# A planned attention kernel: a latest end per slot for fillers and products with v, and eight more homes for VectorE's exponentials

## The chip, the cores and the metric

The kernel runs on one core of one Trainium2 chip. The metric is the device time of one execution in microseconds (us). The engines are TensorE (PE in the profile), VectorE (DVE), ScalarE (ACT), GpSimd (POOL) and SyncE (SP), which issues most DMAs.

## The reference

The inputs are x (2048 x 640), wqkv, wo, w1, b1, w2 and gate_w, all bf16. The layer mixes a 32-head softmax attention (head size 20) with a dense Mish layer by a gate for each row:

```python
g = sigmoid((x * gate_w).sum(-1, keepdims=True))
a = softmax_attention(x, wqkv, heads=32, scale=20 ** -0.5) @ wo
h = x @ w1 + b1
b = (h * tanh(softplus(h))) @ w2
out = g * a + (1 - g) * b
```

## The kernel before, in words

Scores are computed transposed: for a chunk of 512 queries (four chunks c), a group of four heads (eight groups g) and a tile of 128 keys (sixteen tiles kt), each head j gives one unit, a 128 x 512 tile of scores. There are 2048 units in an order that is fixed by `groups`: chunks 0 and 1 alternate group by group, then come chunks 2 and 3. The last group is cut in two halves of 256 queries.

Three units make a slot, and there are 683 slots. The scores of a slot fill three PSUM banks, and two such sets of banks alternate, so the scores of slot s+2 (`emit_s`, matmuls on line 1061) can start once ScalarE has read slot s. ScalarE takes the exponential of a whole slot in one instruction (`emit_e`, line 1083) into one of five ETS buffers. In some slots the third unit is not ScalarE's: VectorE computes its exponential by a polynomial in four instructions (`emit_x`: line 1111 reads the scores, then two on line 1127 and one on line 1129). Such a slot has a narrow instruction on ScalarE (1024 columns instead of 1536); the dictionary `off` holds these slots. The result of such a unit lies in a *home* until TensorE has multiplied it by v. `home()` picks the one that has been free for longest, out of three in a work area of W2R or REG, two in XE and, early on, four lent ones in HB and XS (`LENT`). `ei(home)` gives the address of one. `choose(s)` decides for each slot whether VectorE takes its third unit: not if there is no free home, if VectorE is too far behind, or if its result would come too late for its group; the first slot that may be chosen for is set by `CALM`.

TensorE also makes the products with v (`pv`, line 1197), which add up in the bank ACC, one pass for each key tile; `emit_pv` issues them in order, at most two passes in a step. In between come tasks that share the bank FB: projections for K, Q and v (lines 541, 607, 705, 732), the two matrices of the dense layer (lines 851 and 910), the output projection (line 934), and a check of the score range (line 774). They are cut into single matmuls and run by due times; those called forced must be through by their due step. At the end `spin` (line 1471) and `repeat_s` add matmuls without a purpose where TensorE would stand too idle (`fill_up`). Normalised results of chunks 0 and 1 lie in the tile OTN, those of chunks 2 and 3 in the columns of QT that are no longer needed.

No order on any engine is decided on the chip. A planner in Python (class `Plan`) adds one instruction after the other with an assumed cost, keeps a clock for each engine, and derives the waits from the dependencies. The main loop goes slot by slot: forced tasks, the exponential of the slot, the scores of slot s+2, fillers for the clock, VectorE's unit, then products with v, then tasks up to `limit`, then fillers again. In this loop `limit` is the time by the planner's clock until which tasks may run:

```python
limit = pl.now["act"] + EXP + HOP if step < NSLOT else 1e9
owed = min(owed + rate, 1.0) if step < NSLOT else 1e9
...
emit_pv(step, 2 if step < NSLOT - 1 else 99)
```

`emit_pv` itself knew no limit in time. A second program for large scores is built behind a flag and does not run with these inputs.

Of the kernel before, what the change touches and what calls it, by code (L numbers as in the profile page):

```python
# [10 lines left out]
I32 = mybir.dt.int32  # L11
# [36 lines left out]
SWITCH = 0.1  # L48
COL = 1 / 2400.0
PASS = CW * COL  # L50
EXP = 1.335
STREAM = 0.48
SPUN = 0.6
EXP_PAIR = 0.908
# [24 lines left out]
LAG = 9  # L79
SPARE = 3.5  # L80
WINDOW = 3.41
CALM = 4
PACKED = 10
PACKED_Q = 12
Q_AT = 100
# [3 lines left out]
H_AT = 150  # L89
H_STEP = 12.5  # L90
THIN = 0.09
OVER = 0.2
CUTS = ((0, 256), (256, 256))

# [124 lines left out]
def bass_gated_mix__softmax_full_mha__dense_activation_mish__prompt_kernel(  # L219
# [35 lines left out]
    OTN = sb("OTN", [P, 2, NG, CW], BF16)  # L255
# [26 lines left out]
    def ball(tb):  # L282


        at = XS[:, :] if tb < 2 else XB[:, (tb - 2) // 4, (tb - 2) % 4 // 2 * 2 * D:][:, 0:2 * D]
        return at[:, (tb % 2) * D:(tb % 2 + 1) * D]
# [23 lines left out]
    def ei(home):  # L310

        area, b = home
        if area == "h":
            return HB[:, 1, 4 * b:4 * b + 4, :].rearrange("p f t -> p (f t)").bitcast(I32)
        if area == "x":
            return XS[:, 0:2 * CW].bitcast(I32)
        return XE[:, b - 3, :] if b >= 3 else AREAS[area][1][:, b * CW:(b + 1) * CW]

    def otn(c, g, fast):
# [14 lines left out]
    NSLOT = -(-NC * NG * NKT * HG // SLOT)  # L334


    off = {}
    off_units = {}

    def attention(pl, fast):  # L340
# [3 lines left out]
        at = {}  # L344
# [80 lines left out]
        def flush(done):  # L425

            while not done():
                ready = [lane for lane in soon if lane]
                first = min(ready, key=lambda lane: (lane[0][2]().t1 if lane[0][2] else 0.0, lane[0][3]))
                first.popleft()[1]()  # L430
# [24 lines left out]
        otn_read = {0: [], 1: []}  # L455
# [493 lines left out]
        def of(half):  # L949
            return slice(half * HALF, (half + 1) * HALF)  # L950
# [18 lines left out]
        def p_task(c, t, half, due, rest=False):  # L969

            tb = c * 4 + t
            some = late if rest else every
            needed = [g for g in some if g < NG - 1]
            needed.append(next((k[1] for k, (at, w) in cut.items() if k[0] == c and at <= t * P < at + w), NG - 1))

            def ready():
                if any((c, g) not in otn_done for g in needed) or (fast and (tb, half) not in bdone):
                    return None
                if fast and len(wog_ready) < 2 * HG + 1 or rest and (t, half) not in part_done:
                    return None  # L980
                return [otn_done[(c, g)] for g in needed] + wog_ready

            def finish(bank, last):
                otn_read[c % 2].append(last)
                add = PART[:, t, half, :] if rest else ball(tb)[:, of(half)]
                if rest:
                    ev = mix(ended(t, half), bank, tb, add, [last, part_done[(t, half)]])
                    give(t, half, ev)
                    return ev
                ev = mix(OUTT[:, :], bank, tb, add, [last, bdone.get((tb, half)), *out_dma.values()])  # L990
                store(tb, half, ev)
                return ev

            return Task([p_mm(c, t, half, g, some) for g in some], HALF * COL, finish, due, ready)
# [22 lines left out]
        ei_free = {(a, b): None for a in range(2) for b in range(3)}  # L1017
        ei_free.update({(None, b): None for b in range(3, UNITS)})
        ei_free.update({at: None for at in LENT})
        given_back = set()  # L1020
        area = [0]
        nx = [0]
        off_home = {}
# [2 lines left out]
        started = {}  # L1026
        queue = deque()
        hold = {"until": 0}
        acc_free = [m_acc if fast else pl.add("dve", lambda e: e.memset(PS[:, ACC, :], 1.0))]

        def compose(s, extra=None):
# [19 lines left out]
        def score_mms(s, some, deps):  # L1051

            op = None
            for r in range(max(len(subs(*u[:3])) for u in some)):
                began = False
                for i, (c, g, kt, j) in enumerate(some):
                    if r >= len(subs(c, g, kt)):
                        continue
                    tile, cols, of_q = subs(c, g, kt)[r]
                    cost = max(extent(c, g)[1] * COL, THIN)  # L1060
                    op = pl.add("pe", lambda e, i=i, g=real(g), tile=tile, j=j, cols=cols, c=c, of_q=of_q: e.matmul(  # L1061
# [36 lines left out]
        def home():  # L1098

            some = [(None if b >= 3 else area[0], b) for b in range(UNITS)]  # L1100
            some += [at for at in LENT if at[0] not in given_back]
            some = [at for at in some if ei_free[at] != "busy"]
            return min(some, key=lambda at: ei_free[at].t1 if ei_free[at] else 0.0, default=None)

# [98 lines left out]
        def emit_pv(step, passes):  # L1203

            while passes and step >= hold["until"]:
                if not queue:
                    return
                c, g, kt, _ = queue[0][2]
                emit_off((c, g), False)
                n = HG - sum(u[2] == kt for u in off_units.get((c, g), ()) if fast)  # L1210
                if len(queue) < n:
                    return
                if kt == tiles(c, g) - 1 and not emit_off((c, g), True):
                    if step < NSLOT - 1:
                        return
                    flush(lambda: emit_off((c, g), True, True))
                passes -= 1
                some = [queue.popleft() for _ in range(n)]
                lasts = pv([(u, ETS[:, s % NETS, i, :], [e_op[s]]) for s, i, u in some])
                for k, (s, i, u) in enumerate(some):  # L1220
                    op = pv_slot[s] = lasts[k]
                    pv_left[s] -= 1
                if kt == tiles(c, g) - 1:
                    hold["until"] = step + PV_HOLD
                    group_done(c, g, step, op)
# [70 lines left out]
        if fast:  # L1296
# [60 lines left out]
            for make, args in rest:  # L1357
                t = make(*args, 0)
# [131 lines left out]
        for step in range(NSLOT + 40):  # L1490
            now["step"] = step
            if step >= NSLOT and not queue and not tasks and not any(k >= step for k in at):
                break

            for t in [t for t in tasks if t.forced and t.due <= step]:
                while now["open"] not in (None, t):
                    put(now["open"])
                while t in tasks:
                    put(t)
            if step < NSLOT:  # L1500
                emit_e(step)
            if fast and area[0] and not w2_load and len(h_done) >= FIRST and all(ei_free[(0, b)] != "busy" for b in range(3)):
                load_w2()
            if acts and safe(acts[0][0]) < pl.now["act"] and mish_free():
                acts.popleft()[1]()
            ahead = able = 0.0
            rate = behind = 0.0
            lag = max((step - t.due for t in tasks if not t.forced and t.ready() is None), default=0)
            for t in tasks:
                slack = max(1, t.due - AHEAD * t.forced - step)  # L1510
                ahead += t.left()
                rate = max(rate, ahead / slack)
                if t.forced or t is now["open"] or t.ready() is not None:
                    able += t.left()
                    behind = max(behind, able / slack)
            now["rate"] = rate
            if step + 2 < NSLOT:
                compose(step + 2, choose(step + 2) if fast and step >= CALM and (step < slot_of(0, 1, 0) or behind < CATCH_UP and (lag < LAG or backlog() < SPARE) and room()) else None)
                emit_s(step + 2)
                to_come = pv_ready() * PASS  # L1520
                if owed + rate > 0.1 and pick(pl.now["pe"] + 0.8):
                    to_come += min(owed + rate, 0.4)
                fill_up(to_come, False)

                if fast and step + 2 in off:
                    emit_x(step + 2)
            limit = pl.now["act"] + EXP + HOP if step < NSLOT else 1e9
            owed = min(owed + rate, 1.0) if step < NSLOT else 1e9
            if fast and step < NSLOT and now["open"] and now["open"].left() <= min(owed + OVER, limit - pl.now["pe"] - PASS - SWITCH):
                t = now["open"]  # L1530
                while t in tasks:
                    put(t)
                    owed -= t.cost
            emit_pv(step, 2 if step < NSLOT - 1 else 99)

            while owed > 0:
                t = pick(limit)
                if t is None:
                    break
                put(t)  # L1540
                owed -= t.cost
            fill_up(0.0, True)
            for fn in at.pop(step, []):
                fn()
            work(pl.now["act"] + 0.5 if step < NSLOT else 1e9)
        assert not queue and not tasks and not bg and not any(soon) and not norm and not blend and not acts, (len(queue), len(tasks), len(bg), len(acts))

        c = NC - 1
# [109 lines left out]
    fast = Plan("f_")  # L1658
# [55 lines left out]
```

## Time and profile before

| what | value |
|---|---|
| median of 3 runs | 866.54 us (866.3 to 866.74) |
| the profiled execution | 866.43 us |
| its span, first to last instruction | 864.6 us |
| TensorE busy | 756.3 us (87%) |
| VectorE busy | 829.4 us (96%) |
| ScalarE busy | 847.8 us (98%) |
| wide exponentials (128 x 1536) | 454 |
| narrow exponentials (128 x 1024) | 229, of which 228 by VectorE's units and one the last, short slot |
| products with v, score matmuls, spins | 1875 on ETS, 2202, 103 |

Busy time is the union of an engine's instructions. A releaser, written `<-`, is what ended an engine's idle time just before an instruction. The profiled execution's own time is 1.8 us above its span.

### The profile page before, as it was taken

Reading aid. Unit: us, or ns where it says so; the run is one execution under the profiler, and the core shown is the slowest. Engines: PE = TensorE matmul, PEld = TensorE weight load, DVE = VectorE, ACT = ScalarE, POOL = GpSimd, SP = SyncE. Lnnn points to the kernel's source line nnn. Section 1 sums busy time; section 2 is a strip of 40 time slices with the busy share of each in tenths; the row PEclk is TensorE's granted clock in tenths of the full one; section 3 lists DMA queues with packets and bytes.
Section 4 is the critical chain, followed back from the end, with each engine's and each line's share of the span. In section 5 each row is a group of like instructions: output and inputs, shape, how many; then the busy total and the mean of one; then the engine's idle time right before and its main releaser. Section 6 shows DMA issues by size and latency. Waiting matters only on the chain.

```text
span 864.6 us, 15494 instructions
## 1 busy us (share of the span) xinstructions
PE 756.3 (87%) x6342; PEld 259.5 (30%) x6342; DVE 829.4 (96%) x1330; ACT 847.8 (98%) x714; POOL 7.3 (1%) x14
## 2 busy tenths in 40 slices
PE   8988998889889888898888888898888888899886
PEld 3333332223322332232223333333322333333232
DVE  4799999999999999999999999999999999999996
ACT  6999999999999999999999999999999999999996
POOL 2000000000000000000000000000000000000000
PEclk9999999999999999999999999999999999999999
DMA  9711310012233221401111211112112211000001
GB/s 215 95 61 36 107 46 19 16 60 69 78 93 89 67 62 53 123 26 38 44 39 44 71 34 58 44 36 60 55 44 60 59 51 41 28 25 29 18 14 35
DMA packets 76318, 48.42 MB, mean 56 GB/s; under 512 B 22104, under 2 KB 71888, under 8 KB 76192
## 3 DMA queue, kind: packets, MB, share of 16 engines
q1 hardware_dynamic: 73872, 46.86, 20.1%
q8 instruction: 52, 0.85, 0.4%
q10 hardware_dynamic: 2256, 0.47, 0.3%
q0 software_dynamic: 112, 0.01, 0.1%
q14 instruction: 26, 0.21, 0.1%
HBM read 37.64 MB, written 7.52 MB: 52 GB/s over the span
## 4 chain that ended last, share of the span: by engine, by line
ACT 94%; PE 4%; DMA 1%; DVE 0%; issue 0%; SPq 0%
ACT ETS L1083 92%; ACT REG L884 2%; PE PS L1061 1%; PE PS L1197 1%; ACT W2R L884 1%; DMA OTN<-in_A_x_dram 1%; PE PS L607 0%; PE PS L910 0%; PE PS L670 0%; DVE HB L940 0%; PE PS L774 0%; PE PS L679 0%; PE PS L851 0%; PE PS L541 0%; PE PS L1471 0%
## 5 line engine op out<-in xcount | busy, mean ns | idle before, releaser
L1083 ACT ACTIVATE ETS<-PS 128x1536 bf16<-128x1536 f32 (+1 forms) x683 | 827.6, 1449 | 1.9 <-PE PS L1061 1.7
L1061 PE MATMUL PS<-QT,KT 32*128 32x512 bf16 (+1 forms) x2202 | 275.8, 377 | 95.3 <-ACT ETS L1083 82.7
L1197 PE MATMUL PS<-ETS,V_all 128*21 128x512 bf16 (+1 forms) x1875 | 212.3, 379 | 0.7 <-DVE OUNG L1275 0.4
L1061 PEld LDWEIGHTS PS<-QT,KT 32*128 32x128 bf16 x2202 | 68.4, 91 | 308.9 <-ACT ETS L1083 280.8
L1127 DVE SCALAR_TENSOR_TENSOR ER<-ER 128x512 f32<-128x512 f32 x114 | 77.9, 683 | 0.1
L1127 DVE SCALAR_TENSOR_TENSOR EM<-EM 128x512 f32<-128x512 f32 x114 | 77.7, 682 | 0.0
L1197 PEld LDWEIGHTS PS<-ETS,V_all 128*21 128x21 bf16 x1875 | 48.4, 89 | 92.9 <-issue 84.6
L910 PE MATMUL PS<-W2R,HB 128*128 128x320 bf16 x384 | 74.4, 302 | 0.4
L1111 DVE TENSOR_SCALAR REG<-PS 128x512 f32<-128x512 f32 x85 | 58.2, 685 | 1.9 <-PE PS L1061 1.0
L851 PE MATMUL PS<-XB,REG 128*128 128x256 bf16 x360 | 57.5, 275 | 1.5 <-DVE HB L861 0.9
L1111 DVE TENSOR_SCALAR XE<-PS 128x512 f32<-128x512 f32 x78 | 53.3, 686 | 5.3 <-PE PS L1061 4.3
L910 PEld LDWEIGHTS PS<-W2R,HB 128*128 128x128 bf16 x384 | 28.1, 97 | 38.6 <-issue 27.4
L851 PEld LDWEIGHTS PS<-XB,REG 128*128 128x128 bf16 x360 | 27.9, 97 | 29.1 <-issue 27.2
L861 DVE TENSOR_TENSOR HB<-PS,B1T 128x512 bf16<-128x512 f32 x48 | 32.8, 684 | 1.1 <-PE PS L851 0.9
L1471 PE MATMUL PS<-KT 128*128 128x512 bf16 x103 | 32.0, 385 | 0.0
L1127 DVE SCALAR_TENSOR_TENSOR EM<-REG 128x512 f32<-128x512 uint16 x43 | 29.4, 684 | 0.3
L1129 DVE SCALAR_TENSOR_TENSOR REG<-EM,REG 128x512 int32<-128x512 f32 x43 | 29.3, 681 | 0.0
L1127 DVE SCALAR_TENSOR_TENSOR ER<-REG 128x512 f32<-128x512 uint16 x42 | 28.7, 684 | 0.2
L1129 DVE SCALAR_TENSOR_TENSOR REG<-ER,REG 128x512 int32<-128x512 f32 x42 | 28.6, 681 | 0.0
L1127 DVE SCALAR_TENSOR_TENSOR EM<-XE 128x512 f32<-128x512 uint16 x39 | 26.8, 686 | 0.3
L1127 DVE SCALAR_TENSOR_TENSOR ER<-XE 128x512 f32<-128x512 uint16 x39 | 26.7, 686 | 0.3
L1129 DVE SCALAR_TENSOR_TENSOR XE<-EM,XE 128x512 int32<-128x512 f32 x39 | 26.6, 683 | 0.1
(136 smaller groups left out, 813.1 us busy)
## 6 DMA issues: line engine op xcount, KB each, us to landing
REG<-in_B_w_dram SPq DMA_DIRECT2D x36, 320.0 KB, 3.1
BCT<-SUMS SPq DMA_DIRECT2D x31, 256.0 KB
W2R<-in_B_w_dram SPq DMA_DIRECT2D x12, 320.0 KB, 3.2
KT<-KS SPq DMA_DIRECT2D x28, 128.0 KB
QT<-QS SPq DMA_DIRECT2D x112, 20.0 KB
QS<-WOQ SPq DMA_DIRECT2D x16, 128.0 KB, 1.7
KS<-OTN SPq DMA_DIRECT2D x16, 128.0 KB, 1.7
W2R<-in_B_w_dram SPq DMA_DIRECT2D x1, 1920.0 KB, 9.2
```

The costliest lines, as they stand in the source:

```text
L851: return lambda e, bank: e.matmul(PS[:, bank, i * HW:(i + 1) * HW], w1b(n1)[:, f, i * P:(i + 1) * P], xt(c)[:, f, cols], start=(f == 0), s ...
L861: ev = dve(lambda e: e.tensor_tensor(hb, PS[:, bank, :].rearrange("p (i t) -> p i t", i=2), bias, ALU.add), [last, b_load, *guarded, *b_re ...
L884: ex = pl.add("act", lambda e: e.activation(U, h, AF.Tanh, scale=0.5, bias=-MISH_AT / 2), [ev, u_free[0]], cost=0.95)
L910: return lambda e, bank: e.matmul(PS[:, bank, 0:HALF], HB[:, hc % 2, f, t * P:(t + 1) * P], W2[:, f, half * HALF:(half + 1) * HALF], start ...
L1061: op = pl.add("pe", lambda e, i=i, g=real(g), tile=tile, j=j, cols=cols, c=c, of_q=of_q: e.matmul(scores(s)[:, i, cols], KT[32 * j:32 * j ...
L1083: e_op[s] = pl.add("act", lambda e: e.activation(ETS[:, s % NETS, 0:n, :], scores(s)[:, 0:n, :], AF.Exp, scale=SCALE, bias=LIFT if fast el ...
L1111: ev_op[s] = dve(lambda e: e.tensor_scalar(y, scores(s)[:, 2, :], SCALE * ULPS, BIAS, ALU.mult, ALU.add), [s_op[s], ei_free[b], *(wkv_read ...
L1127: piece(WIDE, lambda e, v=m if i else f, i=i: e.scalar_tensor_tensor(m, v, STEPS[i], v, ALU.add, ALU.mult), lambda i=i: () if i else [lane ...
L1129: piece(WIDE, lambda e: e.scalar_tensor_tensor(x, m, LAST_STEP, y, ALU.mult, ALU.add))
L1197: lasts[n] = pl.add("pe", lambda e, tile=tile, h=real(g) * HG + j, j=j, src=src[:, cols], of_q=of_q, count=count: e.matmul(PS[32 * j:32 * ...
L1471: pl.add("pe", lambda e: e.matmul(PS[:, bank, :], k[:, 0:P], k, start=True, stop=True), [free], cost=PASS, kind="S")
```

## The change

Three edits are made together. `CALM` goes from 4 to 3, so VectorE's units may be chosen one step earlier. A new variable `latest` is set in each step to the planner's time at which the two exponentials after this one will have ended, less `REFILL` = 0.58 us; `limit` is cut to it, and `emit_pv` stops before a pass that would end later. Once all eight output projections of chunk 0 (or 1) have read its half of OTN, four areas in this half join the homes, as `("o", b)`.

```diff
-CALM = 4
+CALM = 3
...
+REFILL = 0.58
...
+        if area == "o":
+            return OTN[:, b // 4, b % 4 * 2:b % 4 * 2 + 2, :].rearrange("p g t -> p (g t)").bitcast(I32)
...
             def finish(bank, last):
                 otn_read[c % 2].append(last)
+                if fast and c < 2 and len(otn_read[c]) == 8:
+                    gained.extend(("o", 4 * c + i) for i in range(4))
+                    ei_free.update({at: last for at in gained[-4:]})
...
+        gained = []
...
+        latest = [1e9]
...
             some += [at for at in LENT if at[0] not in given_back]
+            some += gained
...
+                if passes < 50 and pl.now["pe"] + PASS + (SWITCH if pl.kind != "V" else 0) > latest[0]:
+                    return
                 passes -= 1
...
             limit = pl.now["act"] + EXP + HOP if step < NSLOT else 1e9
+            latest[0] = 1e9
+            if fast and step + 2 < NSLOT:
+                latest[0] = pl.now["act"] + sum(EXP_PAIR if s in off else EXP for s in (step + 1, step + 2)) - REFILL
+                limit = min(limit, latest[0])
```

In the program as built, ScalarE has 228 narrow exponentials instead of 229, VectorE 227 units instead of 228, 52 of them with a home in OTN; TensorE has 21 score matmuls fewer and one spin more, and the same products with v and tasks; the counts of DMAs are the same.

## The prediction

> **What bounds the kernel.** I read the page first.
>
> ```profile
> span 864.6 us, 15494 instructions
> ...
> PE 756.3 (87%) x6342; PEld 259.5 (30%) x6342; DVE 829.4 (96%) x1330; ACT 847.8 (98%) x714; POOL 7.3 (1%) x14
> ...
> ACT 94%; PE 4%; DMA 1%; DVE 0%; issue 0%; SPq 0%
> ```
>
> ScalarE (ACT) is busy for 98% of the span and carries 94% of the chain that ended last. So the time is ScalarE's work, plus what ScalarE loses to others, plus some 10 us ahead and 9 behind. Next the chain of waits in order of time, for the ends of the exponential stream, and ScalarE's groups with shapes kept apart.
>
> ```profile
> 10.33 8.17 ACT ETS L1083 x6
> ...
> 412.27 1.45 ACT ETS L1083
> ...
> 855.99 0.04 issue
> ...
> 859.10 1.00 DVE HB L940 x2
> ```
>
> ```profile
> L1083 ACT ACTIVATE ETS<-PS 128x1536 bf16<-128x1536 f32 x454 | 649.3, 1585 | 1.2 <-PE PS L1061 1.0
> L1083 ACT ACTIVATE ETS<-PS 128x1024 bf16<-128x1024 f32 x229 | 252.5, 1181 | 0.7 <-PE PS L1061 0.7
> L884 ACT ACTIVATE REG<-HB 128x1024 f32<-128x1024 bf16 x18 | 21.5, 1193 | 0.0
> L884 ACT ACTIVATE W2R<-HB 128x1024 f32<-128x1024 bf16 x6 | 7.1, 1178 | 0.0
> ```
>
> The mean durations are not the price of one: neighbours overlap. ScalarE's timeline around twelve wide exponentials in a row gives the price.
>
> ```profile
> 671.04 1.11 ACT L884 ACTIVATE REG<-HB 128x1024 f32<-128x1024 bf16 x1
> 671.99 16.28 ACT L1083 ACTIVATE ETS<-PS 128x1536 bf16<-128x1536 f32 x12
> 687.96 1.25 ACT L884 ACTIVATE REG<-HB 128x1024 f32<-128x1024 bf16 x1
> ```
>
> The first row ends at 672.15, the second at 688.27: 16.12/12 = 1.343 us from end to end. From start to start it is only (687.96-671.99)/12 = 1.331; starts creep ahead of ends. The third row ends at 689.21, so a mish step costs 0.94. For the narrow one I take a run of 50 without a break (its timeline row, then its counts by shape):
>
> ```profile
> 108.07 59.16 ACT L1083 ACTIVATE ETS<-PS 128x1536 bf16<-128x1536 f32 x50 [0.29 <-PE PS L1061]
> ```
>
> ```profile
> L1083 ACT ACTIVATE ETS<-PS 128x1536 bf16<-128x1536 f32 x31 | 46.8, 1653 | 0.3 <-PE PS L1061 0.3
> L1083 ACT ACTIVATE ETS<-PS 128x1024 bf16<-128x1024 f32 x19 | 22.8, 1250 | 0.0
> ```
>
> After a gap a wide one takes 1.45 by itself (the row at 412.27), so 59.16 - 1.45 - 30 x 1.343 = 17.42 for 19: 0.917 each. A narrow one is a slot whose third tile VectorE computes; it spares ScalarE 1.343 - 0.917 = 0.426 us.
>
> The stream runs from 10.33 to 855.99, 845.66 us. Its work is 454 x 1.343 + 229 x 0.917 + 24 x 0.94 = 842.3, with 0.1 for one small instruction; the first exponential starts fresh, another 0.1. So ScalarE loses about **3.2 us** to TensorE in the whole span, and no more can be won by removing late scores. Of it, 1.9 - 0.5 (before the first) = 1.4 is shown as idle in the two group rows, some nine restarts at 0.11 each (1.45 - 1.343) are 1.0, and the rest is slots that start only slightly late.
>
> That ends and not starts count, I checked against the Trainium skill, Perfetto Trace Analysis, section "DVE / Act Engine Instruction": a reported end is where the semaphore update is pushed, a start only where the ALUs begin. The trace agrees, since score groups start 0.05 us after an end (below). By the starts the stream would have lost about 10 us.
>
> **Where the 3.2 us arise.** One loss in the timeline of all engines, then TensorE's timeline around another.
>
> ```profile
> 106.46 1.33 ACT L1083 ACTIVATE ETS<-PS 128x1024 bf16<-128x1024 f32 x1
> ...
> 107.63 0.60 PE L1061 MATMUL PS<-QT,KT 32*128 32x512 bf16 x6
> ...
> 108.07 4.13 ACT L1083 ACTIVATE ETS<-PS 128x1536 bf16<-128x1536 f32 x3 [0.29 <-PE PS L1061]
> ...
> 109.58 0.39 PE L1061 MATMUL PS<-QT,KT 32*128 32x512 bf16 x3 [0.36 <-ACT ETS L1083]
> ```
>
> ```profile
> 583.10 0.39 PE L1061 MATMUL PS<-QT,KT 32*128 32x512 bf16 x3 [0.50 <-ACT ETS L1083]
> 583.42 0.40 PE L1197 MATMUL PS<-ETS,V_all 128*21 128x512 bf16 x4
> 583.74 0.72 PE L851 MATMUL PS<-XB,REG 128*128 128x256 bf16 x5
> 584.40 0.39 PE L1061 MATMUL PS<-QT,KT 32*128 32x512 bf16 x3
> ```
>
> In the first, two narrow exponentials have just passed; scores start at 107.63, the exponential 0.44 later at 108.07, ending the first of its three at 109.52; the next scores follow that end by 0.05. Loss: the three end at 112.20, the one before ended at 107.79, and 4.41 - 3 x 1.343 = 0.38.
>
> This gives a rule. Scores of slot b can start when the exponential of b-2 has ended, and no loss arises if they start 0.44 + 1.45 = 1.89 ahead of the time at which the exponential of b would end in an unbroken stream. Between the starts of the scores of b-1 and b there may then lie: the two exponentials b-2 and b-1, plus one wide (1.343), less 1.89, less 0.05. With one narrow and one wide that is 1.66 us, after a **pair** of narrow ones 0.917 x 2 + 1.343 - 1.94 = **1.23 us**. TensorE's rows: a score group 0.32 to the next instruction, a pass with v 0.32, five filler matmuls 0.66. The second fence is such a pair with all three: 584.40 - 583.10 = 1.30, a loss of 0.07.
>
> I laid this on TensorE's order of instructions as built, with these durations. Before: 77 pairs, 21 overfull, excess 2.3 us; no gap that isn't behind a pair is overfull. Carrying lateness on through runs of three and four gives 2.9 of the 3.2.
>
> **The change, part by part.**
>
> *The latest end* (REFILL). A product pass with v and a filler are now refused where they would end later than the two next exponentials less 0.58 us. The rule above puts the point at 2 x 0.917 + 1.343 - 1.89 = 1.29 after the earlier exponential, where the cap has about 2 x 0.91 - 0.58 = 1.24: the cap lies just inside. What is refused is done one slot later. TensorE has the room:
>
> ```profile
> PE PS L1061 <- ACT ETS L1083: 82.7, 226, 1.1
> ```
>
> It waits 82.7 us for ScalarE in 226 places. Queued behind a refused pass are the later passes with v and through them the reuse of the five ETS buffers; ScalarE's waits name only L1061, never L1197, so that cover exists now. SP, GpSimd and the DMAs keep their counts.
>
> In the changed order I find 65 pairs, 2 overfull, excess 0.5 us: one at the start, one near slot 171. The first is also there now:
>
> ```profile
> 20.39 0.82 PE L541 MATMUL PS<-XB,REG 128*128 128x512 bf16 x3
> ...
> 21.58 2.39 ACT L1083 ACTIVATE ETS<-PS 128x1024 bf16<-128x1024 f32 x2 [0.33 <-PE PS L1061]
> ```
>
> It is a K task with a due step, which the cap does not touch; its 0.33 + 0.11 stays. So the walk falls from 2.9 to 0.5: **-2.4**. Of the 0.3 that the walk does not explain I take half: **-0.1**, between 0 and -0.3.
>
> *CALM 4 to 3.* The choice of a unit may begin a step earlier. In the new order the first four narrow slots stand behind five wide ones instead of six, and their number is the same, so it moves only the opening; between -0.4 (the whole loss at 21.58) and +0.4 (as much again); I take 0.
>
> *More homes.* Eight areas of 128 x 512 words in the tile OTN join the pool, four as soon as the output projection (L934) of a chunk has read its half.
>
> ```profile
> L934 PE MATMUL PS<-WOQ,OTN x128: 299/299/311, 449.7 to 613.0; 128*128 128x320 bf16 x128
> ```
>
> They come free between these times. A unit is one L1111, which takes it from the scores, and three more instructions of the same size:
>
> ```profile
> L1111 DVE TENSOR_SCALAR REG<-PS 128x512 f32<-128x512 f32 x85 | 58.2, 685 | 1.9 <-PE PS L1061 1.0
> ```
>
> With OTN as home no such row exists; the nearest is the one with REG, 685 ns, and I take that; VectorE isn't on the chain, so a few ns either way move nothing by themselves. In the new order 52 of the units live in OTN. But units are not won by it: 227 instead of 228, since three edits together move every later choice. One slot fewer is narrow: **+0.43** on ScalarE. The homes buy spacing: 12 fewer pairs, counted above.
>
> *Fillers for the clock.* 21 score matmuls fewer (17 wide, 4 half; the repeats are among them) and one spin more, on TensorE, beside ScalarE. The tail behind 855.99 hangs on VectorE's last normalisation and the last projections, in the same order in both; four of five spins leave it, and one earlier projection with its eviction (L940, half a us by the row at 859.10) comes into it, ahead of the last three. Between 0 and +0.5; I take 0, as it stands where VectorE waits for TensorE anyway.
>
> Sum: -2.4 - 0.1 + 0.43 = **-2.1 us**. The profiled execution took 866.43 (its span and 1.8 around it), the median of three is 866.54, 0.1 more. I give 864.4, as 866.43 less 2.1 is 864.3 and the median stands 0.1 above. Own range: the unexplained part, the opening and 0.2 of spread make it 863.8 to 865.1.
>
> **Rivals.**
>
> *Half comes back.* What is refused makes a later slot overfull, or a fetch of keys lands late where the order has moved. For it: the sum rests on a walk in which all durations are medians, and 0.3 us of the present loss escapes it. Against it: the 82.7 us of room. Half of 2.5 and the lost slot: -0.8, 865.7.
>
> *It doesn't do what it says*: the caps bind where ScalarE isn't late. Then only the lost slot counts, 867.0. The counted pairs speak against it.
>
> *Slower, by passes with v.* If deferred passes reach the fifth slot, ScalarE waits for an ETS buffer. Each such wait costs a pass, 0.32, and needs passes put off over four slots. At 65 pairs, one in four would be 16 x 0.32 = 5.1, net +3.0, 869.5; it decides from seven such waits on (7 x 0.32 = 2.2 against 2.1). Against it: no wait on L1197 now; by the walk the tightest buffer is read 0.05 us ahead of its reuse in the new order, 0.26 in the old, so it is near in one place, not in seven.
>
> *Slower, by the clock.* Thinner filling may drop TensorE's clock. At half clock a slot's work, near 744.9/707 = 1.05 us busy, grows to about 2 against ScalarE's 842.3/707 = 1.19, some 0.8 us lost per slot; three slots cost 2.4, which eats the gain: 866.8.
>
> ```profile
> 10.30:856.00 845.70, 744.91 (x6279) 254.28 (x6277) 821.17 (x1314) 844.28 (x708) 1.63 (x4) 1.00 0.20 55
> ```
>
> The stream's stretch: its length, busy time and count of TensorE, weight load, VectorE, ScalarE and GpSimd, then the granted clock, 1.00, and the DMAs. In the new order the thinnest three slots hold TensorE work for 0.48 of ScalarE's time (0.54 before), at one place. The Trainium skill, TensorE: Matmul & The Clock Gate, "What's actually happening", makes half rate the default after an idle window of about 3.4 us; no run so far shows such a drop inside the stream.
>
> *Starts count after all*: then 8 us more could go. The 0.05 us speaks against it.
>
> **The numbers.** Forecast 0.73, half back 0.15, without effect 0.03, slower by v 0.03, by the clock 0.03, starts 0.03. A measurement of this kernel can tell about 0.2%, 1.7 us, from no change, so the line lies at 864.8, inside the forecast's own range. Of 0.73 I put 0.63 below it; with the starts' rival faster is 0.67. Same is the 0.10 left, 0.15 and a part of "without effect", 0.27; slower 0.06. Range 863.5 to 866.0: the forecast's own, a little beyond it below, and the half-back case above.
>
> **What would show it.** Right: ScalarE's idle before L1083 falls from 1.9 to about 1.0 us, the gap at 21.58 stays, narrow exponentials are 228 for 229, the chain no longer steps to TensorE between 100 and 375 us. Wrong: waits of L1083 for L1197, a PEclk below 9, or late scores at new places.

## The result and the profile after

The changed kernel takes a median of 870.3 us (867.14 to 873.45, 12 runs), the kernel before 866.7 us (865.86 to 868.24, 12 runs) beside it: the ratio is 1.0042, interval 1.0029 to 1.0054. It is slower by 3.6 us where 864.4 was forecast, and lies above the top of the range, 866.0. The profiled execution took 869.45 us; executions of up to 873.45 us were timed but not profiled.

First the page of the changed kernel: span and instructions, busy time, the granted clock in 40 slices of 21.7 us, and the chain's shares.

```profile
span 867.6 us, 15454 instructions
...
PE 757.3 (87%) x6322; PEld 259.2 (30%) x6322; DVE 828.0 (95%) x1326; ACT 847.2 (98%) x714; POOL 7.2 (1%) x14
...
PEclk9999989999999999999999999999999999999999
...
ACT 91%; PE 3%; DMA 2%; DVE 2%; SPq 1%; issue 0%; ACTq 0%
```

ScalarE's busy time is smaller than before (847.2 against 847.8), yet the span is 3.0 us longer: the time went into waiting. The clock has an 8 in the sixth slice (108 to 130 us), and the chain, which inside the stream stepped only to TensorE before, now holds DMAs, VectorE and SyncE's queue. ScalarE's groups with shapes apart, then four rows of the waits (total, times, longest):

```profile
L1091 ACT ACTIVATE ETS<-PS 128x1536 bf16<-128x1536 f32 x455 | 669.5, 1702 | 2.6 <-PE PS L1069 2.6
L1091 ACT ACTIVATE ETS<-PS 128x1024 bf16<-128x1024 f32 x228 | 270.8, 1280 | 2.5 <-PE PS L1069 2.5
```

```profile
ACT ETS L1091 <- PE PS L1069: 5.1, 8, 1.7
DVE OTN L1254 <- DMA BCT<-SUMS: 3.5, 1, 3.5
PE PS L735 <- DVE OTN L619: 2.5, 1, 2.5
DVE RR L1293 <- DMA RR<-OUNG: 2.4, 3, 1.4
```

The exponentials (L1083 before, L1091 now) are 455 and 228, as counted beforehand; but the idle time ahead of them rose from 1.9 to 5.1 us, where about 1.0 was expected. Eight waits make it, the longest of 1.7 us, and behind them stand waits of VectorE for transfers. By the ends of exponentials, slot by slot (counted from 0), the stream loses 5.4 us in seven places: 0.44 in slot 9 (the K task that was forecast to stay), 0.51 in slot 31, and 4.45 in slots 84 to 88. The many small losses that the forecast meant to remove are gone: before, there were 24 places with 3.27 us together, and none of them but the first is left. The stream runs from 10.33 to 858.58, 848.25 us, 2.6 more than before: 0.43 for the narrow slot fewer, and 2.2 more loss. The last 0.4 of the 3.0 lie behind the stream (9.0 us instead of 8.6).

**Slots 84 to 88.** The changed kernel's timeline of all engines:

```profile
108.79 0.39 PE L1069 MATMUL PS<-QT,KT 32*128 32x512 bf16 x3
110.30 0.69 DVE L1254 TENSOR_TENSOR OTN<-OUNG,BCT 128x512 bf16<-128x512 f32 x1 [3.49 <-DMA BCT<-SUMS]
110.91 0.68 DVE L619 CAST OTN<-PS 128x512 bf16<-128x512 f32 x1
...
111.65 1.07 PE L735 MATMUL PS<-REG,XB 128*128 128x160 bf16 x13 [2.47 <-DVE OTN L619]
...
113.09 1.02 ACT L1091 ACTIVATE ETS<-PS 128x1024 bf16<-128x1024 f32 x1 [1.68 <-PE PS L1069]
...
113.88 0.61 PE L1069 MATMUL PS<-QT,KT 32*128 32x512 bf16 x3
```

VectorE stands 3.49 us at L1254, which normalises an earlier group and reads BCT, the reciprocals of the row sums, spread over the partitions by a DMA (256 KB). Its next instruction is the eviction L619, which frees the PSUM bank that TensorE's next task, a projection for v (L735), needs. So TensorE stands 2.47 us, the next scores are late, and ScalarE waits 1.68. Before, the same instruction (there L1243) stood right behind an eviction (there L616):

```profile
107.19 0.69 DVE L616 CAST OTN<-PS 128x512 bf16<-128x512 f32 x1
108.00 0.69 DVE L1243 TENSOR_TENSOR OTN<-OUNG,BCT 128x512 bf16<-128x512 f32 x1
```

The eviction ends at 107.88, and the last semaphore update of BCT is at 107.97. So VectorE had been idle for 0.12 us even there: there was no room left. Now BCT lands at 110.28, 2.3 us later, and VectorE, done with its work at 106.81, has come 1.1 us earlier; together that is the longer wait.

The last row of the changed kernel's timeline shows a second cost: the same three score matmuls take 0.61 us instead of 0.39. The windows (length, busy time and count of TensorE, weight load, VectorE, ScalarE, GpSimd, then the granted clock, the DMAs' share, GB/s) say why:

```profile
109.59:113.00 3.41, 1.35 (x17) 1.00 (x18) 2.70 (x5) 1.83 (x2) 0.00 (x0) 1.00 0.12 40
113.00:119.82 6.82, 6.63 (x33) 1.17 (x30) 5.75 (x10) 4.86 (x4) 0.00 (x0) 0.50 0.11 38
```

For 6.82 us from 113.0 on TensorE has half its clock, and ScalarE is busy in only 4.86 of them. The five slots lose 1.78, 0.53, 0.96, 0.70 and 0.48 us: the first to the wait, the other 2.67 during and just behind half clock. The split goes by time; no run here has the long stall without the drop.

**Why BCT is late.** SyncE issues all these DMAs from one queue, in order. Its rows before, then after (issue time, time on the queue):

```profile
90.96 0.35 SPq L577 DMA_DIRECT2D KS<-OTN  x1
91.35 1.11 SPq L598 DMA_DIRECT2D KT<-KS  x2
...
93.22 1.07 SPq L598 DMA_DIRECT2D KT<-KS  x2
96.93 0.35 SPq L577 DMA_DIRECT2D KS<-OTN  x1
...
99.77 1.11 SPq L598 DMA_DIRECT2D KT<-KS  x2
100.92 0.52 SPq L1288 DMA_DIRECT2D BCT<-SUMS  x1
```

```profile
90.56 1.11 SPq L601 DMA_DIRECT2D KT<-KS  x2
91.72 0.47 SPq L580 DMA_DIRECT2D KS<-OTN  x1
...
96.48 1.07 SPq L601 DMA_DIRECT2D KT<-KS  x2
97.60 0.47 SPq L580 DMA_DIRECT2D KS<-OTN  x1
...
102.31 1.10 SPq L601 DMA_DIRECT2D KT<-KS  x2
103.46 0.52 SPq L1299 DMA_DIRECT2D BCT<-SUMS  x1
```

At 91 us the write of keys to DRAM (KS<-OTN) and a pair of fetches of earlier keys (KT<-KS) have changed places. The write now lands behind two fetches, and the next pair of fetches, which reads what it wrote, waits for it at the head of SyncE's queue (96.48 instead of 93.22); the write behind that pair is as slow, and everything behind comes later, the issue of BCT by 2.5 us. In the chain of waits of the changed kernel:

```profile
91.72 4.74 DMA KS<-OTN
...
97.60 4.70 DMA KS<-OTN
...
103.46 6.82 DMA BCT<-SUMS
110.30 0.69 DVE OTN L1254
```

Before, the first of these writes took 2.25 us to land and the second 2.82. The planner could not see the difference: it counts 2.0 us for the landing of any such write (`TAIL["sp"]`) and 4.7 for BCT (`tail=4.7`), whatever fetches stand ahead. SyncE's own waits add it up, before and then after:

```profile
SPq L598 <- DMA KS<-OTN: 11.4, 10, 2.0
```

```profile
SPq L601 <- DMA KS<-OTN: 20.1, 9, 3.8
```

### The profile page after: what moved, and what is told of

The parts are those of the page before. It is cut to its first block, busy times and chain, and to the rows that moved or that the text cites. A ratio compares the mean times of both kernels' runs of the same rounds, so it can differ in the third digit from the quotient of the medians.

```text
span 867.6 us, 15454 instructions
## 1 busy us (share of the span) xinstructions
PE 757.3 (87%) x6322; PEld 259.2 (30%) x6322; DVE 828.0 (95%) x1326; ACT 847.2 (98%) x714; POOL 7.2 (1%) x14
## 4 chain that ended last, share of the span: by engine, by line
ACT 91%; PE 3%; DMA 2%; DVE 2%; SPq 1%; issue 0%; ACTq 0%
ACT ETS L1091 88%; ACT REG L887 2%; DMA KS<-OTN 1%; DMA BCT<-SUMS 1%; SPq L601 1%; ACT W2R L887 1%; PE PS L1069 1%; PE PS L610 1%; PE PS L499 1%; DMA RR<-OUNG 1%; DVE EM L1136 0%; DVE ER L1136 0%; PE PS L1206 0%; PE PS L673 0%; DVE HB L943 0%
## 5 line engine op out<-in xcount | busy, mean ns | idle before, releaser
L1091 ACT ACTIVATE ETS<-PS 128x1536 bf16<-128x1536 f32 (+1 forms) x683 | 830.4, 1561 | 5.1 <-PE PS L1069 5.1
L1206 PE MATMUL PS<-ETS,V_all 128*21 128x512 bf16 (+1 forms) x1876 | 208.6, 380 | 0.2
L1206 PEld LDWEIGHTS PS<-ETS,V_all 128*21 128x21 bf16 x1876 | 48.4, 89 | 93.4 <-issue 85.7
L1120 DVE TENSOR_SCALAR XE<-PS 128x512 f32<-128x512 f32 x56 | 38.4, 686 | 3.1 <-PE PS L1069 2.1
L1120 DVE TENSOR_SCALAR REG<-PS 128x512 f32<-128x512 f32 x54 | 36.8, 685 | 1.8 <-PE PS L1069 0.5
L1120 DVE TENSOR_SCALAR OTN<-PS 128x512 f32<-128x512 f32 x52 | 35.5, 682 | 1.1 <-PE PS L1069 0.5
L735 PE MATMUL PS<-REG,XB 128*128 128x160 bf16 (+1 forms) x240 | 23.9, 235 | 3.1 <-DVE OTN L619 2.5
L610 PE MATMUL PS<-XB,WOQ 128*128 128x512 bf16 x80 | 25.5, 399 | 0.3 <-DVE V_all L745 0.2
L937 PE MATMUL PS<-WOQ,OTN 128*128 128x320 bf16 x128 | 24.8, 302 | 0.5 <-DVE HB L864 0.5
L937 PE MATMUL PS<-WOQ,QT 128*128 128x320 bf16 x128 | 24.7, 302 | 0.6 <-DVE QT L1279 0.4
L610 PE MATMUL PS<-XB,REG 128*128 128x512 bf16 x80 | 24.6, 384 | 0.2 <-DVE WOQ L619 0.2
L1120 DVE TENSOR_SCALAR W2R<-PS 128x512 f32<-128x512 f32 x33 | 22.5, 685 | 1.5 <-PE PS L1069 1.1
```

What stands on the lines that cost most here:

```text
L610: return lambda e, bank: e.matmul(PS[:, bank, :], W[:, f, base:base + P], xt(c)[:, f, :], start=(f == 0), stop=(f == NFT - 1))
L937: return lambda e, bank: e.matmul(PS[:, bank, 0:HALF], otn(c, g, fast)[:, t * P:(t + 1) * P], WOG[:, g, half * HALF:(half + 1) * HALF], st ...
L1091: e_op[s] = pl.add("act", lambda e: e.activation(ETS[:, s % NETS, 0:n, :], scores(s)[:, 0:n, :], AF.Exp, scale=SCALE, bias=LIFT if fast el ...
L1120: ev_op[s] = dve(lambda e: e.tensor_scalar(y, scores(s)[:, 2, :], SCALE * ULPS, BIAS, ALU.mult, ALU.add), [s_op[s], ei_free[b], *(wkv_read ...
L1206: lasts[n] = pl.add("pe", lambda e, tile=tile, h=real(g) * HG + j, j=j, src=src[:, cols], of_q=of_q, count=count: e.matmul(PS[32 * j:32 * ...
```

## The experiments

In the edits `fast.ops` is the planned list of operations; `kr` is a fetch of keys, `kw` a write of keys, and nr0, nr1, nr2 are RR<-OUNG, SUMS<-RR and BCT<-SUMS. Moving a DMA in the list moves it in SyncE's queue only.

**Is it the exchange in SyncE's queue?** The changed kernel with the pair of fetches put back behind the write:

```
+    i = next(n for n, op in enumerate(fast.ops) if op.key == "kr00")
+    j = next(n for n, op in enumerate(fast.ops) if n > i and op.key == "kw10")
...
+    fast.ops = fast.ops[:i] + fast.ops[i + 2:j + 1] + fast.ops[i:i + 2] + fast.ops[j + 1:]
```

> The changed kernel with one edit to SyncE's order alone: the first pair of key fetches that stood ahead of a key write (KS<-OTN) is put behind it, as in the kernel before; every other engine keeps its order. Theory (a late broadcast, started by that order, stops VectorE, then TensorE, and the idle TensorE loses its clock): VectorE's wait for BCT at 107 to 110 us falls from 3.5 us to under 1, TensorE's 2.5 us of idle there goes, the granted clock stays at 1.00 up to 856 us, and the time is 864 to 865, some 2 us under the kernel before. Rival (the clock falls because the cap leaves TensorE too thin): the time stays at 868 to 872 and the clock under 0.997.

Measured: 865.14 us (864.3 to 870.0, 12 runs), 0.9987 of before (0.9973 to 1.0001). Its timeline:

```profile
107.60 0.69 DVE L1254 TENSOR_TENSOR OTN<-OUNG,BCT 128x512 bf16<-128x512 f32 x1 [1.01 <-DMA BCT<-SUMS]
```

The wait fell from 3.49 to 1.01 us, the clock stays at 1.00 there, and the stream's loss falls from 5.4 to 1.12. So another order of one write and two fetches is worth about 5 us (5.2 between the medians of the two sessions, 4.8 by the two ratios to before). But four of its 12 runs took 866.8 to 870.0 us, each with a mean clock of 0.992 to 0.995 where the eight others show 0.996 or more: something near the edge is left.

The mirror, the kernel before with nothing but this exchange:

```
...
+    j = max(n for n, op in enumerate(fast.ops) if n < i and op.key == "kw10")
...
+    fast.ops = fast.ops[:j] + fast.ops[j + 1:i + 2] + [fast.ops[j]] + fast.ops[i + 2:]
```

> The mirror: the kernel before, with the same key write put behind that pair of fetches in SyncE's order, nothing else. Theory: the broadcast comes 2 to 3 us later, VectorE waits 2 to 3 us for it near 109 us, TensorE idles 2 us, ScalarE loses 1.5 to 2 us, and with the clock at half for one or two stretches the time is 869 to 873. Rival (the cap): no change, 866.7.

Measured: 870.54 us (869.36 to 871.61, 5 runs), 1.0043 (1.003 to 1.0056). Its timeline and waits show the same event, at other instructions:

```profile
110.22 0.69 DVE L1243 TENSOR_TENSOR OTN<-OUNG,BCT 128x512 bf16<-128x512 f32 x1 [2.87 <-DMA BCT<-SUMS]
```

```profile
PE PS L1061 <- DVE V_all L742: 3.0, 1, 3.0
ACT ETS L1083 <- PE PS L1061: 4.9, 7, 2.4
```

Slots 85 and 86 lose 2.49 and 1.13 us, and the clock is halved for one stretch of 3.41 us. So the exchange alone is enough to make the old kernel as slow as the new one.

**Which edit makes the exchange?** The latest end alone (CALM 4, no homes), and CALM 3 alone, the other edits' conditions set to False:

> The latest end alone (CALM 4, no new homes). Theory: it is this edit that turns the two DMAs round, so the event near 108 us is there, with the clock drop, 869 to 873. Rival (CALM or the homes move the order): no event, about 865.

> CALM 3 alone. Theory: no event near 108 us, the clock holds, late scores as before in 15 or so pairs; 865 to 867. Rival (CALM turns the DMAs round): 869 to 873.

Measured: the latest end alone 870.98 us (870.34 to 871.47, 4 runs), 1.0047 (1.0032 to 1.0061); CALM alone 865.83 (865.24 to 867.84, 10 runs), 0.9988 (0.9979 to 0.9997). With the latest end alone SyncE issues the pair at 90.60 and the write at 91.75, VectorE waits 4.0 us for BCT and half clock lasts 6.8 us. So this edit makes the exchange. How, is read from the code and the traces, not tested by itself: `fetch` is called three steps after the last write that it needs, while a write follows the eviction of a task, and tasks can be put off by the cap. The last eviction ahead of this write starts at 89.78 (89.75 in the changed kernel, 89.38 before), although the one ahead of that comes 0.4 us earlier than before. CALM alone leaves the order of DMAs and the late scores (19 places, 3.2 us); of its gain of about 1 us the profile shows 0.4, one narrow exponential more (230) and a stream shorter by as much; the rest is not explained.

The homes alone, and the latest end alone with the exchange undone:

> The eight homes in OTN alone (CALM 4, no latest end). Theory: the order up to 450 us is that of the kernel before, no event near 108 us, the late scores stay; 866 to 867. Rival (writing units to OTN costs something by itself): slower than 867.5.

> The latest end alone, with the exchange of the first experiment. Theory: the late scores go, the narrow slots fall by a few (it has 225), so 865.5 to 866 where the clock holds. Rival (the cap by itself drops the clock): 869 and more as without the exchange.

Measured: homes 867.03 us (866.46 to 869.24, 10 runs), 1.0005 (0.9996 to 1.0014), its losses 3.4 us, about as before: nothing. The latest end with the exchange undone: 866.38 (865.9 to 872.56, 10 runs), 1.0005 (0.999 to 1.002), 0.4 above what was expected. Its losses did fall to 1.1 us, but it has only 225 narrow exponentials: 4 fewer cost 4 x 0.43 = 1.7 of the 2.2 won. By itself the cap earns nothing that these runs can tell from no change, even without the exchange; the narrow slots come back only with the other edits (226 with the homes, 228 with CALM 3 as well).

**What makes the remaining runs long?** One reading is that BCT is still near the edge, since it lands behind fetches. Then moving four more fetches (`kr10`, `kr11`, `kr20`, `kr21`) behind BCT should quiet both kernels:

```
...
+    j = next(n for n, op in enumerate(fast.ops) if n > i and op.key == "nr2")
+    held = [op for op in fast.ops[i:j] if op.key in ("kr10", "kr11", "kr20", "kr21")]
+    fast.ops = fast.ops[:i] + [op for op in fast.ops[i:j + 1] if op not in held] + held + fast.ops[j + 1:]
```

> The changed kernel with the exchange of the first experiment and, besides, the next four key fetches put behind the broadcast (BCT<-SUMS) in SyncE's order; they are first needed 15 us later. Nothing else moves. Theory (only the late broadcast stood between the change and its forecast): the broadcast lands some 3 us ahead of VectorE's use, no run drops the clock near 108 us, the median is 864.5 and the spread under 1.5 us. Rival (a second cause, the thinner TensorE, still costs the clock in some runs, as in four of twelve of the first experiment): some runs stay at 867 to 870 with a clock under 0.996.

> The kernel before with the same four key fetches put behind the broadcast; nothing else. Theory: its broadcast landed just in time, so the median hardly moves (866.2 to 866.9), but the runs above 868 go. Against the run beside it this gives what the change is worth with the queue out of the way: 2 us. Rival (key fetches behind the broadcast help or hurt by themselves): over 0.7 us off 866.7.

Measured: after with both edits 865.27 us (864.22 to 869.13, 12 runs), 0.9987 (0.9976 to 0.9998), 0.8 above the expected median; before with the second 866.45 (866.16 to 867.55, 12 runs), 0.9997 (0.9988 to 1.0005). In the kernel before, runs above 868 us, seen in each session, did not occur in these 12, which is too few to be sure. In the changed one three of 12 are still at 867.1 to 869.1, with clocks of 0.994 and 0.995. In its profiled run BCT lands at 102.71 for a read at 106.27, so lateness of BCT was at most one cause of the long runs.

The second candidate stands in the timelines near 44 us, of the changed kernel and then of this last version:

```profile
44.47 0.25 DVE L1293 RECIPROCAL RR<-RR 128x16 f32<-128x16 f32 x1 [1.44 <-DMA RR<-OUNG]
...
47.12 0.73 PE L777 MATMUL PS<-REG 128*128 128x128 bf16 x10 [1.11 <-DVE OTN L619]
```

```profile
43.98 0.25 DVE L1293 RECIPROCAL RR<-RR 128x16 f32<-128x16 f32 x1 [1.22 <-DMA RR<-OUNG]
```

It is the same pattern in small: VectorE comes to the first reciprocal before its small DMA (8 KB) has landed, its next eviction is late, TensorE idles 1.11 us, and slot 31 loses 0.51. Putting the reciprocal and its DMA behind VectorE's next three instructions removes the wait without touching TensorE's order (the idle time ahead of L777 falls from 0.90 in the last version to 0.16):

```
+    i = next(n for n, op in enumerate(fast.ops) if op.key == "nr1") - 1
+    j = [n for n, op in enumerate(fast.ops) if n > i + 1 and op.eng == "dve"][2]
...
+    fast.ops = fast.ops[:i] + fast.ops[i + 2:j + 1] + fast.ops[i:i + 2] + fast.ops[j + 1:]
```

> The kernel of the fifth experiment with one more exchange, on VectorE: the first reciprocal of the softmax sums (L1293), which waited 1.2 to 1.4 us near 44 us for the load of the sums (RR<-OUNG), is put behind the three instructions that followed it. Theory (this early wait, which holds an eviction and so TensorE for 0.9 to 1.1 us, is what still drops the clock in a quarter of the runs): the late score near 49 us goes, 0.3 us; the median is 864.3 to 864.8 and no run goes over 866. Rival (the drops come from elsewhere, such as TensorE being thinner in general): two to four of twelve runs stay at 867 to 870.

> The kernel of the fifth experiment once more, beside the two others on the same chip, as their measure: 864.3 to 865.3 for most runs and some at 867 to 869 where the clock drops.

Measured in one session: with this third edit **864.64 us** (864.05 to 865.69, 11 runs), **0.9973** (0.9965 to 0.9982); without it, run again, 864.98 (864.0 to 868.14, 12 runs), 0.9985 (0.9975 to 0.9995), four of the 12 at 866.3 to 868.1. None of its 11 runs is above 866 us, against seven of 24 without the edit; with counts so small chance is not excluded. It beats the kernel before by 0.27%, and the changed one by more. The waits of its ScalarE:

```profile
ACT ETS L1091 <- PE PS L1069: 0.8, 2, 0.5
```

Only slot 9's 0.44 is left as a loss; the stream takes 843.30 us, 2.35 less than before. That the long runs held the early event grown large wasn't seen in a trace, since none of them was profiled. There is a rival: the profiled run without the third edit had a drop of the clock elsewhere, near 419.5 us, at a stretch where TensorE merely has little work. It cost 0.14 us in all, but what makes the other runs long stays open.

**Does CALM 3 matter beside the others?** The changed kernel with CALM 4 and the first two edits to the queue:

> The changed kernel with CALM back at 4, and the queue edits of the fifth experiment. Theory: it has three narrow slots fewer than the changed kernel and VectorE reaches that reciprocal 0.5 us later, so its early wait is short; 865.2 to 865.7 with few or no slow runs. Rival (the slow runs don't hang on the early wait): slow runs as in the fifth experiment.

Measured: 866.75 us (866.15 to 868.35, 11 runs), 0.9998 (0.9989 to 1.0007): a miss, by about 1 us above the upper end. Its losses are as small as expected, 0.6 us. It has 226 narrow exponentials, and its stream takes 844.33 us, 1.0 more than the best version's. The tail, the time behind the stream, is 1.0 longer too (10.4 against 9.4 us). First TensorE waits for the last unit that VectorE computes, then the clock drops (a row of its timeline, then one of its windows):

```profile
855.33 0.39 PE L1206 MATMUL PS<-OTN,V_all 128*21 128x256 bf16 x2 [1.34 <-DVE OTN L1138]
```

```profile
850.00:858.00 8.00, 5.63 (x64) 1.98 (x59) 6.50 (x13) 4.47 (x4) 0.00 (x0) 0.82 0.10 31
```

Two projections (L937) take 0.66 us there, against 0.46 in the best version.

## Why the prediction was wrong

**The step that failed** is a sentence in the part on the latest end: "SP, GpSimd and the DMAs keep their counts." True, and no argument. What counted was the order in SyncE's queue, and the prediction did not compare it, though it was to be had from the programs as built. With "VectorE isn't on the chain" it also took an engine with 829 us of in-order work as free to wait. In fact VectorE had no room at BCT even before (it was idle for 0.12 us there until BCT landed), and behind that read stand the evictions on which TensorE depends. The exchange of one write and one pair of fetches cost about 5 us (870.3 to 865.14; in the mirror +3.4), where the prediction had nothing for it.

**Late scores** were right, in mechanism, place and size. Of 24 late places one was left, the one at 21.58 us that was named; the second that was forecast, near slot 171, shows no loss. The stream's loss went from 3.27 to 0.44 us in the version without stalls, -2.8 against the -2.5 forecast. The rule of pairs (1.23 us between starts) fits this, and the price by ends (1.343 and 0.917) holds: 455 x 1.343 + 228 x 0.917 + 24 x 0.94 + 0.2 = 842.9, and 843.30 was measured for 842.9 + 0.44.

**The narrow slot fewer**, +0.43: confirmed by the counts. **CALM**, costed at 0 with 0.4 to either side: alone it gave 0.3 to 1.8 us by its interval, mostly outside that bound, with 0.4 in the profiled stream; in the joint order it keeps narrow slots (228 against 226). **Homes**: alone nothing, as taken; the spacing that they were said to buy (77 pairs of narrow slots become 69 with them alone) removes no loss by itself. Their price of 685 ns holds (the group with OTN has 682). **The tail**, 0 up to +0.5: +0.4 in the profile of the changed kernel, +0.8 in that of the best version. But two profiles of one kernel (the one with the first two queue edits) have 8.7 and 9.4 us, so one profile does not size this term.

**The rivals.** *Half comes back* named a fetch of keys that lands late. It was the right place, but the price was a share of the gain instead of the length of the stall. *Slower by the clock* had the right consequence: 2.67 us at half clock. It named another trigger, thinner filling, where here a stall of 2.47 us lay ahead, and 0.03 was far too low a chance; a drop behind thin filling is on record too (419.5 us, above), but cost only 0.14. *Slower by v* didn't occur: no wait names L1206. *Without effect* and *starts count* fell with the losses that vanished. Two of the signs of being wrong that it named were there: an 8 in PEclk, and late scores at new places.

With the stalls away, 864.64 us is 2.1 us below before: the sum made in the prediction, for a kernel that is not the one that was run. That the number agrees to 0.1 is partly luck: the profiled spans differ by 1.7 (864.6 to 862.9), the stream 2.35 shorter, its start 0.1 earlier, and the tail 0.8 longer. The time of the changed kernel was thus decided not by the edit's target but by what the reordering did to a queue that the edit doesn't mention.

## What to carry to other kernels

Where a planner orders everything, an edit to one engine's rule changes every queue: lay the old and the new order of each queue side by side, the DMA queue first, and look for a write and a read that have changed places. An engine off the critical chain may have no room where it matters: for each transfer that an in-order engine reads, compare the landing time with the time of the read in the profile, and list what stands behind that read. Compare the landing times that the planner assumes with the measured ones, too. A stall of TensorE should be priced with what its clock does afterwards, not by its length alone.

## What the runs showed of the hardware

When a transfer lands depends on what was issued ahead of it on the same queue: the 128 KB write KS<-OTN landed in 1.7 us alone, in 2.25 with fetches issued just behind it, and in 4.5 to 4.8 just behind two fetches of 128 KB (the changed kernel and the mirror). BCT, 256 KB, took 6.8 to 7.1 us where a pair of fetches stood just ahead of it, and 4.8 where the fetches were held back (97.89 to 102.71, the changed kernel with both edits to the queue). The Trainium skill, DMA: Bandwidth & Descriptors, "Queues, rings and completion order", says that each DMA engine consumes its descriptors in ring order; these numbers agree, and show what it costs a reader that waits.

TensorE's clock fell without 3.41 us of idleness. In the changed kernel the 3.41 us ahead of the drop hold 1.35 us of TensorE work (the first row of the windows above) and no idle piece above 2.47 us, and half clock lasted for two more such stretches, although TensorE was busy in 6.63 of the 6.82 us. In the version without the third edit the clock fell near 419.5 us behind a stretch with 2.04 of 3.41 us busy:

```profile
416.05:419.46 3.41, 2.04 (x21) 0.61 (x19) 3.41 (x6) 3.41 (x4) 0.00 (x0) 0.98 0.34 66
419.46:422.87 3.41, 3.41 (x17) 0.62 (x14) 3.31 (x5) 3.41 (x3) 0.00 (x0) 0.52 0.00 0
```

The Trainium skill, TensorE: Matmul & The Clock Gate, "What's actually happening", has half rate after an idle window of about 3.4 us; the length of the stretches agrees, the need for an idle window does not. Nor does the share of work in a stretch decide alone: the best version has the same matmuls there, 2.03 us in the 3.40 us from 416.0 with the same longest idle piece of 0.92, and its clock stays at 1.00. What decides it stays open, and so does what makes half clock last for one stretch of 3.41 us (the mirror) or two (the changed kernel).
